# Moving part of a kernel's transposes from TensorE to the DMA crossbar: K and Q from pair 5 on, u from batch 1 on

## The chip, the cores and the metric

The kernel runs on one core of a Trainium2 chip. The metric is the device time of one execution in microseconds (us), the median of several runs; lower is better. The kernel before takes 288.5 us (three runs, 288.3 to 289.1). On one core a run is called slow when it is over 1.5% above the fastest of its kernel.

## The reference, cut to what matters

```python
# batch 4, 8 heads, 768 positions, head size 64; d_model 512, d_tok 256, d_ch 1536
scores = q @ k.transpose(0, 1, 3, 2) / 8        # block-sparse mask, softmax over keys
x = softmax(where(mask, scores, -1e9)) @ v      # heads put side by side: 768 x 512 per batch
h = relu(x.T @ w_tok1) @ w_tok2                 # token mixing
u = x + h.T
out = u + relu(u @ w_ch1) @ w_ch2               # channel mixing
```

## The kernel before

Two heads form a pair; there are 16 pairs, four to a batch. QK names the matmuls of the scores, PV those of the softmax with v; the exponentials between them run on ScalarE. Each pair's K and Q arrive with positions on the partitions, and the QK matmuls read them with the head dimension there, so they are transposed: 12 TensorE transposes a pair into PSUM (the memory that the matmuls write), then four copies (evacuations) to SBUF on VectorE or ScalarE. The same is done for u: 24 transposes and four copies a batch. Rows 64 to 87 of the `ktb` and `qtb` tiles hold a mask in low-rank form, which QK adds to the scores.

```python
qtb = [sb1.tile([128, S], BF16, name=f"qtb{n}") for n in range(2 * NV)]   # NV = 4 pairs in flight
ktb = [sb1.tile([128, S], BF16, name=f"ktb{n}") for n in range(2 * NV)]
# ... cut ...
def transposes(p):
    # ... cut: relayout(p) copies the loaded raw tiles into klay and qlay ...
    for nm, bufs, there in (("k", ktb, kT_there), ("q", qtb, qT_there)):
        for c in range(NC):                         # NC = 6 blocks of 128 positions
            def emit(nm=nm, c=c, box=box, rel=rel):
                # ... cut ...
                nc.tensor.matmul(out=box["t"][:, c, :], lhsT=lays[nm][:, c, :, :]...,
                                 rhs=ident[:, :], is_transpose=True, ...)
        for hd in range(2):
            def evac(eng, ...):                     # 64 x 768 out of PSUM, on DVE or ACT
                ...
```

The kernel orders its own instructions. A small planner runs while the program is built. It holds a planned cost for each instruction and a planned landing time for each DMA, plays the engines against each other, and at each step emits the instruction of best priority that would be ready by then. The emitted order is fixed: on the chip each engine takes its instructions in that order and waits at whichever is not ready, even if a later one is.

The softmax here doesn't subtract the row's maximum and nothing guards it: scores larger than these inputs give would overflow.

Of the kernel before, what the change touches and what calls it, by code (L numbers as in the profile page):

```python
# [50 lines left out]
class Planner:  # L51
# [11 lines left out]
    def __init__(self, slots):  # L63
        self.now = 0.0
        self.free_at = {"pe": 0.0, "act": 0.0, "dve": 0.0}
        self.streams = []
        self.ops = []
        self.count = 0
        self.slots = {tag: [Ev(0.0)] * n for tag, n in slots.items()}
        self.exp_pending = 0  # L70
# [6 lines left out]
    def op(self, engines, cost, deps, emit, prio=5, lat=60.0):  # L77
        done = Ev()
        self.ops.append((prio, self.count, engines, cost, deps, emit, done, lat))
        self.count += 1  # L80
        return done
# [21 lines left out]
    def step(self):  # L103

        nxt = []
        moved = False
        if self.free_at["pe"] <= self.now:
            for s in self.streams:
                while s[3] is None or (callable(s[3]) and s[3]()):
                    s[3] = next(s[2], False)  # L110
                if s[3] is False or callable(s[3]):
                    continue
                cost, deps, tags, emit, done = s[3]
                t = self.when(deps, tags)
                if t is None:
                    continue
                if t <= self.now:
                    s[3] = None
                    emit()
                    if self.trace is not None:  # L120
                        self.trace.append((self.now, "pe", s[0], cost))
                    self.free_at["pe"] = self.now + cost
                    if done is not None:
                        done.t = self.now + cost + self.PE_LAT + self.SEM
                    moved = True
                    break
                nxt.append(t)
            self.streams = [s for s in self.streams if s[3] is not False]
        else:
            nxt.append(self.free_at["pe"])  # L130
        for eng in ("act", "dve"):
            if self.free_at[eng] > self.now:
                nxt.append(self.free_at[eng])
                continue
            best = None
            for o in self.ops:
                prio, num, engines, cost, deps, emit, done, lat = o
                if eng not in engines:
                    continue
                if eng == "act" and prio > 0 and self.exp_pending:  # L140
                    continue
                t = self.when(deps)
                if t is None:
                    continue
                if t <= self.now:
                    if best is None or (prio, num) < best[:2]:
                        best = o
                else:
                    nxt.append(t)
            if best is not None:  # L150
                prio, num, engines, cost, deps, emit, done, lat = best
                self.ops.remove(best)
                emit(eng)
                c = cost[eng]
                if self.trace is not None:
                    self.trace.append((self.now, eng, prio, c))
                self.free_at[eng] = self.now + c
                done.t = self.now + c + lat + self.SEM
                moved = True
        if moved:  # L160
            return True
        later = [t for t in nxt if t > self.now]
        if not later:
            return False
        self.now = min(later)
        return True
# [3 lines left out]
def kernel(  # L170
# [22 lines left out]
    NET = 8  # L193

# [14 lines left out]
    qtb = [sb1.tile([128, S], BF16, name=f"qtb{n}") for n in range(2 * NV)]  # L209
    ktb = [sb1.tile([128, S], BF16, name=f"ktb{n}") for n in range(2 * NV)]  # L210

    P = Planner({"ps": 2, "po": 1, "pm": 3, "et": NET, "a_t": 2, "o": 3, "rc": 2,
                 "lay": 2, "kq": NV, "va": NV})
# [112 lines left out]
    rows_there = {("k", n): Ev() for n in range(2 * NV)} | {("q", n): Ev() for n in range(2 * NV)}  # L326

    def mask_stream():
# [15 lines left out]
        for h in range(2):  # L344
            def copy(eng, h=h):
                nc.scalar.copy(out=qtb[0][R, 384 * h : 384 * h + 384], in_=pms[h][R, 0:384])
            e2.append(P.op(("act",), {"act": 420.0}, [done], copy, prio=0))
            rels[h].same_as = e2[h]
        rows_there["q", 0].same_as = e2[1]
        for n in range(2 * NV):  # L350
            for nm, bufs in (("k", ktb), ("q", qtb)):
                if (nm, n) == ("q", 0):
                    continue

                def copy(eng, n=n, nm=nm, bufs=bufs):
                    nc.vector.tensor_copy(
                        out=bufs[n][R, :], in_=indf if nm == "k" else qtb[0][R, :]
                    )
                rows_there[nm, n].same_as = P.op(
                    ("dve",), {"dve": 300.0}, e2, copy, prio=2 if n < 2 else 6  # L360
                )
# [5 lines left out]
    ones_there = [Ev() for _ in range(NV)]  # L367

# [14 lines left out]
    def relayout(p):  # L383
        lays = {}
        for nm in ("k", "q", "v"):
# [3 lines left out]
            def emit(eng, nm=nm, raw=raw):  # L389
                if nm == "v":  # L390
                    nc.vector.tensor_copy(out=vaug[p % NV][:, :, :, 0:64], in_=raw[:, :, :, :])  # L391
                    return
                lay = sbw.tile([128, NC, 2, D], BF16, tag=f"{nm}lay", bufs=2, name=f"{nm}lay{p}")
                nc.vector.tensor_copy(  # L394
                    out=lay[:, :, :, :], in_=raw[:, :, :, :].rearrange("p h c d -> p c h d")
                )
                lays[nm] = lay
# [4 lines left out]
            if nm != "v" and p >= 2:  # L402
                deps.append(qT_there[p - 2, 1])
# [4 lines left out]

    def transposes(p):
        for hd in range(2):  # L410
            kT_there[p, hd], qT_there[p, hd] = Ev(), Ev()
        yield lambda: ("v", p) in raws
        lays = relayout(p)
        for nm, bufs, there in (("k", ktb, kT_there), ("q", qtb, qT_there)):
# [15 lines left out]
            n_left = [2]  # L430
            for hd in range(2):
                buf = bufs[2 * (p % NV) + hd]

                def evac(eng, hd=hd, buf=buf, box=box):
                    i = box["t"][64 * hd : 64 * hd + 64, :, :].rearrange("p c s -> p (c s)")
                    if eng == "act":
                        nc.scalar.copy(out=buf[0:64, :], in_=i)
                    else:
                        nc.vector.tensor_copy(out=buf[0:64, :], in_=i)  # L439
# [17 lines left out]
    def qk_stream():  # L457
        for s in steps:
# [4 lines left out]
            def emit(s=s, done=done, rel=rel):  # L463
# [4 lines left out]
                for hd in range(2):  # L468
                    n = 2 * (p % NV) + hd
                    nc.tensor.matmul(  # L470
                        out=ps[:, hd, 0:384], lhsT=ktb[n][0:88, 128 * j : 128 * j + 128],
                        rhs=qtb[n][0:88, 384 * half : 384 * half + 384], start=True, stop=True,
# [3 lines left out]
                def exp(eng):  # L476
# [13 lines left out]
                [e for hd in range(2) for e in (  # L490
                    kT_there[p, hd], qT_there[p, hd],
                    rows_there["k", 2 * (p % NV) + hd], rows_there["q", 2 * (p % NV) + hd],
# [8 lines left out]
    def pv_stream():  # L501
        for s in steps:
# [3 lines left out]
            def emit(s=s, done=done):  # L506
# [23 lines left out]
                def norm(eng):  # L530
                    if b not in xs:
                        xs[b] = sbw.tile([128, NC, DM], BF16, tag="x", bufs=B, name=f"x{b}")
# [3 lines left out]
                        out=free(xs[b][:, 3 * half, 128 * pb : 128 * pb + 128], 0,  # L536
                                 [[64, 2], [DM, 3], [1, 64]]),
# [29 lines left out]

    def tok(b, g):
# [3 lines left out]
        for t in range(2):  # L572
            for sc in range(NC):
                def emit(t=t, sc=sc):
                    if t == 0 and sc == 0:
# [4 lines left out]
                        rhs=xs[b][:, sc, 256 * g : 256 * g + 256],  # L580
# [4 lines left out]
        if b not in st:  # L585
            st[b] = dict(u=xs[b], uT_there=[Ev() for _ in range(4)])
# [6 lines left out]
        for s2 in range(3):  # L593
# [16 lines left out]
            def add(eng, s2=s2, ubox=ubox):  # L610
                nc.vector.tensor_tensor(  # L611
                    out=st[b]["u"][:, 2 * s2 : 2 * s2 + 2, 256 * g : 256 * g + 256],
                    in0=ubox["pm"][:, :, :],
                    in1=xs[b][:, 2 * s2 : 2 * s2 + 2, 256 * g : 256 * g + 256], op=ALU.add,
# [5 lines left out]
        alias(a_rel, last)  # L620
        for dmc in (2 * g, 2 * g + 1):
            last, rel, tbox = Ev(), Ev(), {}
            for sc in range(NC):
                def emit(sc=sc, dmc=dmc, rel=rel, tbox=tbox):
                    if sc == 0:
                        P.take("pm", rel)
                        tbox["pt"] = psM.tile([128, NC, 128], BF16, tag="pm", name=f"pm_ut_{b}_{dmc}")
                    nc.tensor.matmul(  # L628
                        out=tbox["pt"][:, sc, :], lhsT=st[b]["u"][:, sc, 128 * dmc : 128 * dmc + 128],
                        rhs=ident[:, :], start=(sc == 0), stop=(sc == NC - 1), is_transpose=True,  # L630
                    )
                yield 56.0, [u_evs[sc // 2]], [("pm", 1)] if sc == 0 else [], emit, last if sc == NC - 1 else None

            def evac(eng, dmc=dmc, tbox=tbox):
                if "uT" not in st[b]:
                    st[b]["uT"] = sbw.tile([128, 4, S], BF16, tag="uT", bufs=B, name=f"uT{b}")
                o, i = st[b]["uT"][:, dmc, :], tbox["pt"][:, :, :].rearrange("p c s -> p (c s)")
# [9 lines left out]
    def ch(b, pool, tag):  # L647
# [4 lines left out]
        for cc in range(12):  # L652
            for sh in range(2):
                last, rel, pbox = Ev(), Ev(), {}
                for dmc in range(4):
                    first = dmc == 0
                    def emit(cc=cc, sh=sh, dmc=dmc, rel=rel, pbox=pbox):
                        if dmc == 0:
# [7 lines left out]
                            rhs=st[b]["uT"][:, dmc, 384 * sh : 384 * sh + 384],  # L666
# [11 lines left out]
                rc_there[cc, sh] = ev  # L678
        for sc in range(NC):
# [12 lines left out]
            def fin(eng, sc=sc, pbox=pbox):  # L692
                o = sbw.tile([128, DM], FP32, tag="o", bufs=3, name=f"o{b}_{sc}")
                nc.vector.tensor_tensor(  # L694
                    out=o[:, :], in0=pbox["pm"][:, :], in1=st[b]["u"][:, sc, :], op=ALU.add
# [37 lines left out]
    P.stream(-1, mask_stream())  # L733
    tok2_op = P.op(("dve",), {"dve": 900.0}, [tok2_raw], wtok2_lay, prio=3)
# [57 lines left out]
```

## Time and profile before

| | before |
|---|---|
| time | 288.5 us |
| span of the profiled run | 287.1 us |
| first exponential to last (ScalarE) | 12.0 to 160.9 us |
| last QK matmul to the last matmul | 159.7 to about 283 us |
| TensorE, ScalarE, VectorE busy | 94%, 67%, 45% |

The groups of instructions of the kernel before follow (line, engine, operation, tiles, shapes, count; then busy us and mean ns of one; then idle time of the engine before them and what ended it). The transposes and their copies are many small pieces, and exponentials and QK are the large groups of the attention stage.

```profile
L478 ACT ACTIVATE et<-ps 128x768 bf16<-128x768 f32 x192 | 143.2, 810 | 4.2 <-PE ps L470 3.2
...
L439 DVE COPY ktb<-tk 64x768 bf16<-64x768 bf16 x29 | 16.0, 552 | 17.5 <-PE tk L421 17.2
...
L421 PE MATMUL tq<-ident,qlay 128*128 128x128 bf16 x96 | 11.3, 230 | 0.2 <-DVE qlay L394 0.2
```

### The profile page before, as it was taken

How to read it: one execution, taken by the hardware profiler on the slowest of the kernel's cores; microseconds unless marked ns; L12 is line 12 of the kernel's file. 1: busy time of each engine (PE TensorE's matmuls, PEld its weight loads, DVE VectorE, ACT ScalarE, POOL GpSimd, SP SyncE). 2: the span in 40 equal slices, each digit the busy share in tenths (PEclk: the TensorE clock that was granted, in tenths of full speed). 3: DMA queues.
4: the chain of work that ended last, by engine and by line, in shares of the span. 5: the costliest groups of instructions: out<-in, count | busy, mean ns of one | idle time of the engine just before them, and what ended most of it. 6: DMA issues, size and time to landing. Idle time of an engine off the chain costs nothing.

```text
span 287.1 us, 6351 instructions
## 1 busy us (share of the span) xinstructions
PE 269.9 (94%) x2682; PEld 175.5 (61%) x2690; DVE 130.2 (45%) x286; ACT 191.9 (67%) x286; POOL 45.0 (16%) x70
## 2 busy tenths in 40 slices
PE   0799899999999999999999999999999999999994
PEld 0366676678777777777777754456544654456441
DVE  5789966557777569765546341210022001200121
ACT  1589999999999999999999642037501770067200
POOL 7956554522211000000000000000000000000000
PEclk9999999999999999999999999999999999999999
DMA  4999999996254100000000001220022001210122
GB/s 55 134 204 202 214 201 205 201 185 87 39 73 66 23 2 2 0 2 3 2 0 2 2 0 39 106 76 0 2 110 84 29 0 73 94 54 0 38 102 82
DMA packets 19168, 20.07 MB, mean 70 GB/s; under 512 B 1348, under 2 KB 15428, under 8 KB 19140
## 3 DMA queue, kind: packets, MB, share of 16 engines
q0 software_dynamic: 15648, 13.37, 30.3%
q1 hardware_dynamic: 3492, 6.29, 5.8%
q8 instruction: 21, 0.34, 0.5%
q14 instruction: 7, 0.06, 0.1%
HBM read 26.74 MB, written 6.29 MB: 115 GB/s over the span
## 4 chain that ended last, share of the span: by engine, by line
PE 73%; ACT 14%; DVE 6%; issue 2%; DMA 2%; POOL 2%; POOLq 0%; DVEq 0%; ACTq 0%
PE pm_ch L686 22%; PE pm_ch L664 21%; ACT et L478 14%; PE ps L470 14%; PE po L520 8%; PE pm_tok L578 3%; PE pm_tok L603 2%; DMA kraw<-in_k_dram 2%; DVE qtb L439 1%; PE pm_ut L628 1%; PE tq L421 1%; DVE ktb L439 1%; PE tk L421 1%; DVE x L535 1%; DVE klay L394 1%
## 5 line engine op out<-in xcount | busy, mean ns | idle before, releaser
L478 ACT ACTIVATE et<-ps 128x768 bf16<-128x768 f32 x192 | 143.2, 810 | 4.2 <-PE ps L470 3.2
L470 PE MATMUL ps<-qtb,ktb 88*128 88x384 bf16 x384 | 95.3, 329 | 4.0 <-ACT et L478 1.7
L560 ACT ACTIVATE rc<-pm_ch 128x384 bf16<-128x384 f32 x84 | 41.2, 491 | 60.7 <-PE pm_ch L664 44.8
L520 PEld LDWEIGHTS <-et 128*128 128x128 bf16 x1152 | 56.0, 97 | 22.8 <-DVE x L535 1.9
L664 PE MATMUL pm_ch<-uT,w_ch 128*128 128x384 bf16 x384 | 68.6, 326 | 0.2 <-DVE rc L562 0.2
L686 PE MATMUL pm_ch<-w_ch,rc 128*128 128x512 bf16 x280 | 62.4, 379 | 0.4
L520 PE MATMUL po<-vaug,et 128*128 128x65 bf16 x1152 | 61.5, 193 | 0.5 <-ACT et L478 0.2
L694 DVE TENSOR_TENSOR o<-pm_ch,x 128x512 f32<-128x512 f32 x24 | 16.6, 692 | 98.7 <-PE pm_ch L686 98.7
L664 PEld LDWEIGHTS <-w_ch 128*128 128x128 bf16 x384 | 37.0, 98 | 23.1 <-issue 0.3
L686 PEld LDWEIGHTS <-rc 128*128 128x128 bf16 x288 | 28.2, 98 | 33.6
L470 PEld LDWEIGHTS <-ktb 88*128 88x128 bf16 x384 | 34.2, 99 | 11.9 <-issue 4.4
L439 DVE COPY ktb<-tk 64x768 bf16<-64x768 bf16 x29 | 16.0, 552 | 17.5 <-PE tk L421 17.2
L611 DVE TENSOR_TENSOR x<-pm_tok,x 128x512 bf16<-128x512 f32 x24 | 16.2, 687 | 6.8 <-PE pm_tok L603 6.5
L535 DVE TENSOR_TENSOR x<-po,recip 128x384 bf16<-128x384 f32 x32 | 17.8, 557 | 1.1
L439 DVE COPY qtb<-tq 64x768 bf16<-64x768 bf16 x30 | 16.6, 552 | 2.1 <-PE tq L421 1.1
L603 PE MATMUL pm_tok<-a_t,w_tok 128*128 128x256 bf16 x96 | 17.0, 272 | 0.0
L230 POOL DMA_DIRECT2D vraw<-in_v_dram x16 | 12.3, 766 | 28.4 <-DVE vaug L391 25.7
L578 PE MATMUL pm_tok<-x,w_tok 128*128 128x256 bf16 x96 | 16.3, 272 | 0.0
L230 POOL DMA_DIRECT2D kraw<-in_k_dram x16 | 11.6, 727 | 7.7 <-DVE recip L534 2.2
L230 POOL DMA_DIRECT2D qraw<-in_q_dram x16 | 11.5, 720 | 6.4 <-DMA w_ch<-in_moe_w_ch_dram 2.4
L534 DVE RECIPROCAL recip<-po 128x6 f32<-128x6 f32 x32 | 6.2, 195 | 12.0 <-PE po L520 11.6
L421 PE MATMUL tq<-ident,qlay 128*128 128x128 bf16 x96 | 11.3, 230 | 0.2 <-DVE qlay L394 0.2
(49 smaller groups left out, 122.8 us busy)
## 6 DMA issues: line engine op xcount, KB each, us to landing
out_dram<-o SPq DMA_DIRECT2D x24, 256.0 KB, 2.0
kraw<-in_k_dram POOLq DMA_DIRECT2D x16, 192.0 KB, 7.9
qraw<-in_q_dram POOLq DMA_DIRECT2D x16, 192.0 KB, 7.4
vraw<-in_v_dram POOLq DMA_DIRECT2D x16, 192.0 KB, 7.0
w_ch<-in_moe_w_ch_dram POOLq DMA_DIRECT2D x8, 384.0 KB, 9.8
w_tok<-in_moe_w_tok_dram POOLq DMA_DIRECT2D x1, 384.0 KB, 7.8
w_tok2r<-in_moe_w_tok_dram POOLq DMA_DIRECT2D x1, 384.0 KB, 9.0
samp<-in_sampled_blocks_dram SPq DMA_DIRECT2D x1, 0.6 KB
```

The source lines that it names most:

```text
L230: nc.gpsimd.dma_start(out=raw[:, :, :, :], in_=APx(src, 2 * p * S * D, [[NC * D, 128], [S * D, 2], [1, NC * D]]),)
L421: nc.tensor.matmul(out=box["t"][:, c, :], lhsT=lays[nm][:, c, :, :].rearrange("p h d -> p (h d)"), rhs=ident[:, :], start=(c == 0), stop=( ...
L439: nc.vector.tensor_copy(out=buf[0:64, :], in_=i)
L470: nc.tensor.matmul(out=ps[:, hd, 0:384], lhsT=ktb[n][0:88, 128 * j : 128 * j + 128], rhs=qtb[n][0:88, 384 * half : 384 * half + 384], star ...
L478: nc.scalar.activation(out=et[:, :, :], in_=ps[:, :, 0:384], func=AF.Exp, scale=0.125)
L520: nc.tensor.matmul(out=po[:, hd, c, :], lhsT=et[:, hd, 128 * c : 128 * c + 128], rhs=va[:, hd, j, 0:65], start=(j == 0 and hd == 0 and c = ...
L535: nc.vector.tensor_tensor(out=free(xs[b][:, 3 * half, 128 * pb : 128 * pb + 128], 0, [[64, 2], [DM, 3], [1, 64]]), in0=po[:, :, :, 0:64], ...
L560: nc.scalar.activation(out=o(), in_=i, func=AF.Relu)
L578: nc.tensor.matmul(out=box["pm"][:, t, :], lhsT=w_tok1[:, sc, 128 * t : 128 * t + 128], rhs=xs[b][:, sc, 256 * g : 256 * g + 256], start=( ...
L603: nc.tensor.matmul(out=ubox["pm"][:, i, :], lhsT=w_tok2[:, t, 2 * s2 + i, :], rhs=a_t[:, t, :], start=(i == 0 and t == 0), stop=(i == 1 an ...
L664: nc.tensor.matmul(out=pbox["pm"][:, 0:384], lhsT=w_ch1[:, dmc, 128 * cc : 128 * cc + 128], rhs=st[b]["uT"][:, dmc, 384 * sh : 384 * sh + ...
L686: nc.tensor.matmul(out=pbox["pm"][:, :], lhsT=box["rc"][:, cc, 128 * sc : 128 * sc + 128], rhs=w_ch2[:, cc, :], start=(cc == 0), stop=(cc ...
```

## The change

The intent is to take 204 of the 288 transposes off the full TensorE and their evacuations off VectorE. For pairs 5 to 15 VectorE copies the raw K (and Q) into a "wide" tile whose blocks are 128 columns: 64 of data, 24 of mask constants, 40 of zeros. One crossbar transfer (`dma_start_transpose`, a DMA that transposes on its way) then writes all of `ktb` (or `qtb`) of the pair. There are two wide tiles for each of K and Q, so pair p+2 uses pair p's tiles again. For batches 1 to 3 a crossbar transfer turns each half of u. All 28 transfers are issued by SyncE. The early pairs stay on TensorE; in the kernel before, the input loads fill the DMA engines up to about 65 us (DMA share 1.17 to 1.28 in the windows from 10 to 60 us, 0.67 from 60 to 80, 0.35 from 80 to 100). The core of the diff, cut:

```diff
+    NPE = 5
+    NL = 2
-    qtb = [sb1.tile([128, S], BF16, name=f"qtb{n}") for n in range(2 * NV)]
-    ktb = [sb1.tile([128, S], BF16, name=f"ktb{n}") for n in range(2 * NV)]
+    qtb = [sb1.tile([128, 2, S], BF16, name=f"qtb{n}") for n in range(NV)]
+    ktb = [sb1.tile([128, 2, S], BF16, name=f"ktb{n}") for n in range(NV)]
+    wide = {
+        (nm, n): sb1.tile([128, 2, NC, 128], BF16, name=f"{nm}wide{n}")
+        for n in range(NL) for nm in ("k", "q")
+    }
 ... (relayout)
+                elif p >= NPE:
+                    nc.vector.tensor_copy(out=wide[nm, p % NL][:, :, :, 0:64], in_=raw[:, :, :, :])
 ...
+            if nm != "v" and p >= NPE:
+                deps.append(wide_there[nm, p % NL])
+                if p - NL >= NPE:
+                    deps.append(xb_done[nm, p - NL])
 ...
+    def crossbar(p):
+        lays = relayout(p)
+        for nm, bufs, there in (("k", ktb, kT_there), ("q", qtb, qT_there)):
+            def emit(eng, nm=nm, bufs=bufs):
+                nc.sync.dma_start_transpose(
+                    out=bufs[p % NV][:, :, :].rearrange("e h (c s) -> e (h c) s", c=NC),
+                    in_=wide[nm, p % NL][:, :, :, :].rearrange("p h c e -> p (h c e)"),
+                )
+            deps = [lays[nm + "ev"]]
+            if p >= NV:
+                deps.append(qk_done[p - NV])
+            ev = P.op(("sp",), {"sp": 1500.0}, deps, emit, prio=1, lat=2500.0)
+            xb_done[nm, p] = ev
+            there[p, 0], there[p, 1] = ev, ev
 ... (tok: u)
+        if b > 0:
+            turn_by_crossbar(b, g, u_evs)
+            return
```

The numbers 1500 and 2500 are the planner's own ns for issue and landing of one transfer. The layouts of x, u and uT change with it, so that each half of u is contiguous.

## The prediction

> **What bounds the kernel now.** I read the page's slices first, to see where each engine is busy, then the table of stretches, then groups of instructions, then the order of instructions in time at the places where a stretch looked odd.
>
> The slices of the kernel before, 7.2 us each:
> ```profile
> PE   0799899999999999999999999999999999999994
> DVE  5789966557777569765546341210022001200121
> ACT  1589999999999999999999642037501770067200
> PEclk9999999999999999999999999999999999999999
> DMA  4999999996254100000000001220022001210122
> ```
> TensorE is full from slice 5 to the end at full clock. ScalarE is full only up to about 160 us (the softmax exponentials), the DMA engines only up to about 65 us. So there are two stages: attention, where TensorE and ScalarE are both full, and a tail of channel mixing, where TensorE is alone. The stretches say the same (columns: busy us and instructions of each engine, granted clock, DMA share, GB/s):
> ```profile
> 20.00:40.00 20.00, 18.35 (x244) 13.15 (x244) 17.33 (x40) 19.00 (x26) 11.12 (x16) 1.00 1.22 205
> ...
> 120.00:140.00 20.00, 19.75 (x274) 15.06 (x273) 11.76 (x25) 19.94 (x28) 0.00 (x0) 1.00 0.01 2
> ...
> 180.00:200.00 20.00, 19.95 (x109) 10.58 (x109) 2.77 (x4) 7.37 (x15) 0.00 (x0) 1.00 0.17 66
> ```
> Busy times overlap, so the cost on TensorE is the distance from one start to the next. The order in time on TensorE shows it (start us, length us, ... count):
> ```profile
> 162.34 1.47 PE L578 MATMUL pm_tok<-x,w_tok 128*128 128x256 bf16 x12
> ...
> 167.25 0.61 PE L628 MATMUL pm_ut<-ident,x 128*128 128x128 bf16 x8
> 168.06 6.01 PE L664 MATMUL pm_ch<-uT,w_ch 128*128 128x384 bf16 x36 [0.20 <-DVE rc L562]
> ```
> Eight transposes in 0.61 us of which the last one's 0.219 us is drain: (0.61-0.219)/7 = 56 ns each. In the same way 162.5 ns for a channel-mixing matmul of 384 columns ((6.01-0.326)/35), 109 ns for a token-mixing one of 256, and from like stretches 216 ns for 512 columns, 162 for a QK matmul, 29 for a PV matmul.
>
> In attention, which of the two is ahead? The exponentials' starts are 722 ns apart when nothing holds them (the fourth pair of heads: 12 in 8.68 us), but pairs 6 to 15 take 8.8 to 9.1 us each, 9.03 in the mean: TensorE paces there, by about 0.37 us a pair. In the first 60 us it is the other way round: of TensorE's idle time most lies there, waiting for ScalarE. One hole is worth naming, in ScalarE's order in time:
> ```profile
> 29.79 2.26 ACT L478 ACTIVATE et<-ps 128x768 bf16<-128x768 f32 x3
> 31.96 1.61 ACT L437 COPY ktb<-tk 64x768 bf16<-64x768 bf16 x2
> 33.91 0.80 ACT L437 COPY qtb<-tq 64x768 bf16<-64x768 bf16 x1 [0.33 <-DVE qtb L439]
> 34.99 18.51 ACT L478 ACTIVATE et<-ps 128x768 bf16<-128x768 f32 x25 [0.29 <-PE ps L470]
> ```
> For 2.95 us no exponential runs. VectorE's order in time tells why: the mask row of pair 2's second q buffer, a low-priority copy, is written only at 34.17 us behind the evacuations of later pairs' transposes, and the first QK of pair 2 starts at 34.34.
>
> [...]
>
> **The change part by part.** Numbers of instructions are from the two programs' instruction orders.
>
> Removed from TensorE: 12 transposes for each of 11 pairs (5 to 15) and 24 for each of 3 batches: 132 + 72 = 204, at 56 ns 11.4 us. Added: 12 small matmuls (24 columns) that make the constant columns of the wide tiles, some 0.4 us. Net 11.0 us of TensorE work of 257.6 (all matmuls at the distances above).
>
> Removed from VectorE and ScalarE: 4 evacuations a pair and 4 a batch, 44 + 12 = 56, at 552 ns 31 us, nearly all VectorE's, which isn't the bound. Added there: 4 clears and 4 copies, planned at 420 and 450 ns, 3.5 us around 30 to 40 us. The re-layout copies (371 ns) stay, with another destination.
>
> Moved: the kernel orders its matmuls with a planner of its own, and fills the freed time in attention with channel mixing. After the last QK matmul the program before has 345 first-layer and 288 second-layer channel matmuls, 24 token matmuls, 12 transposes and 18 PV matmuls: 345x0.1625 + 288x0.216 + 24x0.109 + 12x0.056 + 18x0.029 = 122.1 us; the trace has 159.7 to about 283, 123.4 us. The changed program has 288, 278, 24, 0 and 18: 46.8 + 60.0 + 2.6 + 0.5 = 110.0 us. So the tail is 12.1 us shorter by its order alone, unless attention grows.
>
> Attention: its work on TensorE is 1.0 us more than before (136.5 against 135.5), as 57 + 10 channel matmuls (11.4 us) replaced the transposes. By pair:
> - pair 0: same order but for small things, 10.9 us as before.
> - pair 1: before 12.06 us with the hole. In the changed order pair 2's mask rows stand before pair 1's first normalization, and ScalarE evacuates nothing after its first two copies, so the hole should be gone. TensorE has 7.4 us of work; ScalarE's 8.7 rule, with VectorE still crowded: 9.3.
> - pairs 2 to 4: 7.7 to 8.2 us of TensorE work, so ScalarE's pace: 8.75 each, 26.25 (before 26.7).
> - pair 5: 8.57 us of work, 8.85.
> - pairs 6 to 14: 8.99 and 8.87 us of work in turn. The loss over 60 to 160 us is now 3.8 us, 0.34 a pair, part of it at the changes between transposes and QK; I take 0.28: 9.2 each, 82.8. Pair 15: 9.0.
>
> First exponential at 12.0 as before; 12.0 + 10.9 + 9.3 + 26.25 + 8.85 + 82.8 + 9.0 = 159.1, against 160.9 before. The last QK is 1.2 us earlier, 157.9. Tail 110.0 plus 0.6 of waits (before 1.3, with the wait on u's transposes, which goes): 268.5. From there to the end of the measured time it is 288.47 - 283.1 = 5.4 us before, the same after: 273.9. I say 274.2, leaving a little for crossbar disturbance.
>
> Do the crossbar transfers hide? Pair p may start once QK of pair p-4 is done, some 27 us ahead of its use. Batch 3's u is used only after batches 1 and 2, over 60 us later. So latency is hidden; only throughput matters: 22 + 4 transfers between about 35 and 147 us, one per 4.3 us.
>
> **The rivals.**
> 1. The crossbar is slower than one transfer per 4.3 us. The DMA packets of the trace before take 79 ns for 768 B and 86 ns for 2 KB, almost flat: if a transpose goes as 1536 rows of 256 B at some 60 ns over 16 engines, it takes 5.8 us (my estimate), 26 take 150 us where 112 are there, QK waits, and the time goes to 300 us or more. For it: the flat cost. Against it: [...] the kernel's own plan counts 1.5 us of issue and 2.5 of landing, where its other costs (552 against 550 planned, 692 against 695) match the trace closely.
> 2. Loads collide. DMA share is over 1.2 of the page's measure until 65 us, and the first crossbars (pairs 5 to 7) fall into 35 to 50 us. Loads or transposes late by a few us would still be met by the 27 us lead; if not, one stall of 2 to 5 us, 276 to 279.
> 3. ScalarE takes over: it cannot go below 8.66 us a pair, so what TensorE gains in attention beyond the fill is idle. The plan's fill leaves TensorE at 8.9 a pair, so little is lost. If attention kept its length exactly, the time would be 288.5 - 12.1 = 276.4.
> 4. The strided reading of the new u transposes (three runs of 128 columns) slows 384 channel matmuls. [...] At 5% it would cost 3 us.
>
> **Range and chances.** Rivals 2 to 4 give 274 to 279, a cleaner attention stage 271.5. Predicted 274.2 us, 271 to 279. Faster by over 2% (below 282.7) 0.90; within 2% 0.04; slower by over 2% 0.06, nearly all rival 1.
>
> **What would show it.** Right: no exponential gap between pairs 1 and 2; pairs 6 to 14 at about 9.2 us; end of the exponentials near 159; tail from last QK of about 110.5 us; transposes landing within a few us. Wrong: TensorE waiting for a DMA into ktb, qtb or uT; pairs above 9.5 us; channel matmuls with a distance above 163 ns.

The forecast's sum: 159.1 us to the end of the exponentials, so the last QK at 157.9; with 110.0 + 0.6 for the tail 268.5; with 5.4 to the end 273.9, said as 274.2. There is no term for a crossbar transfer in it, since I took the transfers as hidden. What stands against rival 1 is the planner's own 1.5 and 2.5 us; the trace before has no crossbar transfer, so no measured transfer stood against it. The 60 ns of rival 1 is an estimate of mine, set below the 79 and 86 ns that it stands beside. The 0.4 us for the 12 small matmuls was an estimate too; in the trace after they take 0.38 us (36.57 to 36.95).

## More of the kernel before

The chain of work that ended last, by engine, as a share of the span. DMA is almost absent from it:

```profile
PE 73%; ACT 14%; DVE 6%; issue 2%; DMA 2%; POOL 2%; POOLq 0%; DVEq 0%; ACTq 0%
```

## The result, and the profile after

The changed kernel takes 303.6 us (four runs: 301.5, 303.2, 304.0, and 310.3, which counts as slow) against 288.7 us (its four runs). Ratios here and below are the mean time of one kernel's fast runs over that of the other's of the same rounds, so not quite the ratio of the medians: 1.049, interval 1.043 to 1.055. The prediction was 274.2 us with a range to 279: wrong, and in the wrong direction.

The slices of the kernel after, 7.5 us each:

```profile
PE   0799993249897995989999999999999999999994
...
DVE  5689870124462642553545342420012001210021
ACT  1679993219897994889999998006710572047300
...
PEclk9999998559999998899999999999999999999998
DMA  3999999999999997853952002151012101210022
```

TensorE has a hole at slices 6 to 8 (45 to 68 us) and smaller dents up to slice 17, in places where it was full before. ScalarE and VectorE have the hole too, so none of the three was working: they all waited for something else. The only row that is full there is DMA, and it stays full to about 113 us, where before it ended at 65. From slice 18 on the picture is as hoped.

The chain that ended last, by engine, has DMA with 18% of the span where it had 2%:

```profile
PE 67%; DMA 18%; ACT 6%; DVE 4%; POOL 2%; issue 1%; SPq 0%; POOLq 0%; DVEq 0%; ACTq 0%
```

The instructions in order of time on VectorE show who waited (start us, length us, engine, line, operation, tiles, count, then idle time before it and what ended it):

```profile
44.12 0.67 DVE L694 TENSOR_TENSOR x<-pm_tok,x 128x512 bf16<-128x512 f32 x1
55.35 0.36 DVE L432 COPY kwide<-kraw 128x768 bf16<-128x768 bf16 x1 [10.56 <-DMA ktb<-kwide]
55.63 0.68 DVE L694 TENSOR_TENSOR x<-pm_tok,x 128x512 bf16<-128x512 f32 x1
63.53 0.36 DVE L432 COPY qwide<-qraw 128x768 bf16<-128x768 bf16 x1 [7.21 <-DMA qtb<-qwide]
63.80 0.19 DVE L597 RECIPROCAL recip<-po 128x6 f32<-128x6 f32 x1
```

The copy of pair 7's K into its wide tile stands in VectorE's order between two additions for token mixing. It must wait until pair 5's transfer has read the same tile, and so VectorE stands still for 10.6 us, then 7.2 us for Q. The addition and the normalization (the reciprocal) behind the copies were wanted by others. TensorE's order in time in the same stretch:

```profile
47.31 0.28 PE L715 MATMUL pm_ut<-ident,x 128*128 128x128 bf16 x2
56.37 0.29 PE L715 MATMUL pm_ut<-ident,x 128*128 128x128 bf16 x1 [8.78 <-DVE x L694]
...
64.64 0.84 PE L583 MATMUL po<-vaug,et 128*128 128x65 bf16 x12 [6.59 <-DVE x L598]
```

TensorE waits 8.8 us for the addition, then 6.6 us for the normalization, whose PSUM buffer PV needs. Nobody here waits for a `ktb` or `qtb` tile to be filled. Over the whole run VectorE waits 38 us for K and Q transfers, by the view of waits (us in total, times, longest):

```profile
DVE kwide L432 <- DMA ktb<-kwide: 21.0, 6, 10.6
DVE qwide L432 <- DMA qtb<-qwide: 17.0, 6, 7.2
```

Why were the transfers late? SyncE's order in time shows the issues (the length is how long SyncE's queue was held by one issue):

```profile
41.13 4.13 SPq L461 DMA_TRANSPOSE ktb<-kwide  x1
45.32 8.58 SPq L461 DMA_TRANSPOSE qtb<-qwide  x1
54.00 7.71 SPq L461 DMA_TRANSPOSE ktb<-kwide  x1
61.76 5.54 SPq L461 DMA_TRANSPOSE qtb<-qwide  x1
```

The view of the tile qtb between 40 and 62 us, and that of ktb between 128 and 152 us, end with the time from issue to landing of the transfers in that stretch:

```profile
DMA to landing us min/median/max: 11.8/14.9/18.1
```
```profile
DMA to landing us min/median/max: 3.8/3.8/3.8
```

The same transfer lands after 12 to 18 us early on and after 3.8 us later. The profile page's part on DMA queues says what was added (packets, MB, share of 16 engines); q1 carried only the outputs before, 3,492 packets and 5.8%:

```profile
q1 hardware_dynamic: 47396, 17.31, 30.7%
q0 software_dynamic: 15648, 13.37, 29.3%
```

The added 43,008 packets of 256 B are 28 transfers of 1,536 packets each. I counted the packets by start time in the trace's DMA records:

```
stretch of the kernel after   crossbar packets (256 B)   load packets (1024 or 768 B)
45 to 48 us                    449                        461
48 to 51                       476                        453
54 to 57                       562                        560
57 to 60                       586                        550
60 to 63                       560                        556
163 to 168, no loads          1536 in 2.03 us               0
```

In these stretches the two queues go one packet for one. A load packet of 768 B takes 78 ns and one of 1,024 B 96 ns, a crossbar packet 30 ns there (18 in the median without loads, from 163 to 168 us), so a transfer gets some 150 to 195 packets through in a us and lasts 8 to 10 us in place of 2.0: 9.2 and 8.0 us for the first two, from the first packet to the last. The rest of the 12 to 18 us is waiting: the first transfer's packets start 4.0 us after its issue, the second's at 54.3 us, 9.0 us after its issue and right behind the first's last packet. These are counts; that the engines take turns is read from them, and no run varies the turns themselves.

By pairs of heads, from a pair's first exponential to the next pair's, I read the cost of it in the trace:

| pair | before | predicted | after |
|---|---|---|---|
| 0 | 10.9 | 10.9 | 11.7 |
| 1 | 12.1 | 9.3 | 9.1 |
| 2 | 9.0 | 8.75 | 9.3 |
| 3 | 8.7 | 8.75 | 26.4 |
| 4 | 9.0 | 8.75 | 9.0 |
| 5 | 8.9 | 8.85 | 10.4 |
| 6 | 9.0 | 9.2 | 11.2 |
| 7 | 9.1 | 9.2 | 9.5 |
| 8 | 9.1 | 9.2 | 14.5 |
| 9 | 9.0 | 9.2 | 10.1 |
| 10 to 14, mean | 9.0 | 9.2 | 9.05 |

The exponentials end at 187.9 us, 28.8 later than predicted. Pair 3 has 17.6 of that, pairs 5 to 9 another 10. The tail, from the last QK at 186.6 to the end of the last matmul at 297.6, is 111.0 us, as predicted. The last channel-mixing stretches on TensorE look like this:

```profile
204.01 15.76 PE L753 MATMUL pm_ch<-uT,w_ch 128*128 128x384 bf16 x96
```

(15.76 - 0.326)/95 = 162.5 ns between matmuls, the same as before, so the strided reading of the new uT costs nothing.

### The profile page after: what moved, and what is told of

Its sections match the earlier page's. It is cut to its first block, busy times and chain, and to the rows that moved or that the text cites. A ratio compares the mean times of both kernels' runs of the same rounds, so it can differ in the third digit from the quotient of the medians.

```text
span 301.5 us, 6014 instructions
## 1 busy us (share of the span) xinstructions
PE 263.5 (87%) x2498; PEld 167.0 (55%) x2498; DVE 112.0 (37%) x254; ACT 184.5 (61%) x270; POOL 44.8 (15%) x70
## 4 chain that ended last, share of the span: by engine, by line
PE 67%; DMA 18%; ACT 6%; DVE 4%; POOL 2%; issue 1%; SPq 0%; POOLq 0%; DVEq 0%; ACTq 0%
PE pm_ch L776 21%; PE pm_ch L753 19%; PE ps L533 14%; DMA qtb<-qwide 13%; PE po L583 8%; ACT et L542 6%; PE pm_tok L686 3%; DMA qraw<-in_q_dram 2%; DMA ktb<-kwide 2%; PE pm_tok L661 2%; DMA kraw<-in_k_dram 2%; DVE x L598 1%; DVE qwide L432 1%; POOL kraw L236 1%; POOL vraw L236 0%
## 5 line engine op out<-in xcount | busy, mean ns | idle before, releaser
L533 PE MATMUL ps<-qtb,ktb 88*128 88x384 bf16 x384 | 98.6, 339 | 3.0 <-ACT qtb L500 1.6
L583 PEld LDWEIGHTS <-et 128*128 128x128 bf16 x1152 | 57.9, 99 | 38.7 <-DVE x L598 16.3
L583 PE MATMUL po<-vaug,et 128*128 128x65 bf16 x1152 | 63.3, 196 | 13.3 <-DVE x L598 13.3
L753 PE MATMUL pm_ch<-uT,w_ch 128*128 128x384 bf16 x384 | 72.3, 326 | 0.0
L625 ACT ACTIVATE rc<-pm_ch 128x384 bf16<-128x384 f32 x72 | 35.4, 491 | 55.6 <-PE pm_ch L753 55.5
L776 PE MATMUL pm_ch<-w_ch,rc 128*128 128x512 bf16 x288 | 64.6, 379 | 0.0
L533 PEld LDWEIGHTS <-ktb 88*128 88x128 bf16 x384 | 36.1, 101 | 16.2 <-issue 4.7
L694 DVE TENSOR_TENSOR x<-pm_tok,x 128x512 bf16<-128x512 f32 x24 | 15.8, 684 | 12.5 <-PE pm_tok L686 12.5
L236 POOL DMA_DIRECT2D vraw<-in_v_dram x16 | 12.1, 755 | 39.8 <-DVE vaug L430 29.3
L627 DVE TENSOR_SCALAR rc<-pm_ch 128x384 bf16<-128x384 f32 x24 | 13.2, 553 | 11.2 <-PE pm_ch L753 11.1
L432 DVE COPY kwide<-kraw 128x768 bf16<-128x768 bf16 x11 | 4.0, 368 | 21.0 <-DMA ktb<-kwide 21.0
L432 DVE COPY qwide<-qraw 128x768 bf16<-128x768 bf16 x11 | 3.9, 355 | 19.7 <-DMA qtb<-qwide 17.0
## 6 DMA issues: line engine op xcount, KB each, us to landing
w_ch<-in_moe_w_ch_dram POOLq DMA_DIRECT2D x8, 384.0 KB, 10.1
```

The source lines that it names most:

```text
L236: nc.gpsimd.dma_start(out=raw[:, :, :, :], in_=APx(src, 2 * p * S * D, [[NC * D, 128], [S * D, 2], [1, NC * D]]),)
L533: nc.tensor.matmul(out=ps[:, hd, 0:384], lhsT=ktb[n][0:88, hd, 128 * j : 128 * j + 128], rhs=qtb[n][0:88, hd, 384 * half : 384 * half + 38 ...
L583: nc.tensor.matmul(out=po[:, hd, c, :], lhsT=et[:, hd, 128 * c : 128 * c + 128], rhs=va[:, hd, j, 0:65], start=(j == 0 and hd == 0 and c = ...
L625: nc.scalar.activation(out=o(), in_=i, func=AF.Relu)
L694: nc.vector.tensor_tensor(out=st[b]["u"][:, g, 2 * s2 : 2 * s2 + 2, :], in0=ubox["pm"][:, :, :], in1=xs[b][:, g, 2 * s2 : 2 * s2 + 2, :], ...
L753: nc.tensor.matmul(out=pbox["pm"][:, 0:384], lhsT=w_ch1[:, dmc, 128 * cc : 128 * cc + 128], rhs=st[b]["uT"][:, dmc // 2, 3 * sh : 3 * sh + ...
```

## The experiments

My theory after this reading has two parts. A: a late transfer stops VectorE, which stands at a refill of a wide tile, and VectorE's stop stops everyone. D, which the texts name from `e5` on: the loads make the transfers late, packet by packet. The rivals: B, the crossbar's own throughput is the bound, whoever waits; C, the opening is spoiled by the new layouts or by the preparation of the wide tiles; E, the crossbar traffic disturbs the engines' memory access. Eleven kernels ran, ten with correct results and `e9` wrong; all were timed in three rounds, `e10` in five.

### e1_wide4: four wide tiles in place of two

```diff
+    NW = 4
-        for n in range(NL) for nm in ("k", "q")
+        for n in range(NW) for nm in ("k", "q")
-    wide[nm, p % NL] ... wide_there[nm, p % NL]
+    wide[nm, p % NW] ... wide_there[nm, p % NW]
-                o = sbw.tile([128, DM], FP32, tag="o", bufs=3, ...)
+                o = sbw.tile([128, DM], FP32, tag="o", bufs=2, ...)
```

> Edit: the changed kernel with four wide buffers for each of K and Q in place of two (and two output buffers in place of three to make room); order of the planner and all 28 crossbar transfers kept. Theory A (VectorE, in order, stands before the copy that refills a wide buffer until an earlier crossbar transfer has landed, 38 us in the changed kernel, and normalizations and u additions behind it stand too): those VectorE waits on K and Q transfers drop from 38 us to under 8, the 9.3 and 7.3 us gaps of the exponentials in pair 3 go; what is left is QK of pairs 5 to 7 waiting for late landings, 5 to 8 us: time 278 to 284. Rival B (the crossbar's own throughput is the bound, whoever waits for it): QK waits in VectorE's place, time 297 or more.

Measured: 288.1 us, ratio to before 0.997 (0.993 to 1.002): 15.5 us better than the changed kernel, but not the 278 to 284 expected. The gap in pair 3 is gone (8.9 us). VectorE still waits 18.8 us in all for K and Q transfers, and there is a wait that the changed kernel did not have. From the view of waits of this run (engine, line waited for: us in total, times, longest):

```profile
DVE qwide L433 <- DMA qtb<-qwide: 14.2, 4, 5.3
...
PE ps L534 <- DMA qtb<-qwide: 5.9, 2, 3.3
...
DVE kwide L433 <- DMA ktb<-kwide: 4.6, 1, 4.6
```

QK of pair 5 starts at 63.66 us, right behind the landing of pair 5's Q at 63.52; QK of pair 6 at 79.20, behind 79.07. So about half of the loss goes with two more wide tiles. VectorE's first stops, in pair 3, go; what is left comes later, and now QK also waits, because the transfers themselves are too late: the first four land at 55.6, 63.5, 72.3 and 79.1 us, some 8 us apart, where the pairs need two in 9 us. Rival B is right under the loads, and only there: after 110 us this run's transfers land after 4 to 6 us.

### e4_plan_late: only the planned landing time changed

```diff
-            ev = P.op(("sp",), {"sp": 1500.0}, deps, emit, prio=1, lat=2500.0)
+            ev = P.op(("sp",), {"sp": 1500.0}, deps, emit, prio=1, lat=14000.0)
```

> Edit: one number in the kernel's own plan, the landing time that it counts for a K or Q transfer, from 2.5 to 14 us; instructions and transfers the same, only their order differs (the copies that refill wide buffers stand later in VectorE's order). Theory A: the early waits of VectorE (10.6 and 7.2 us) shrink to under 4 us together, time 280 to 290. Rival B (throughput of the crossbar under the loads): no gain, within 2% of the changed kernel's 303.

Measured: 292.7 us, ratio 1.014 (1.011 to 1.017). The same instructions in another order (their counts on each engine are equal in the two traces) are 11 us faster than the changed kernel, so the order alone around the late landings was worth that much. The gap moved rather than vanished: pair 3 takes 8.9 us, but VectorE stops for 6.3, 5.1 and 5.8 us between 57 and 77 us, and pairs 4 and 5 take 14.4 and 21.6 us:

```profile
DVE qwide L432 <- DMA qtb<-qwide: 12.1, 2, 6.3
DVE kwide L432 <- DMA ktb<-kwide: 5.1, 1, 5.1
```

The expected under 4 us of early waits was missed, and the time fell just outside the expected 280 to 290.

### e2_pairs9: the crossbar only from pair 9 on

```diff
-    NPE = 5
+    NPE = 9
```

> Edit: pairs 5 to 8 go back to TensorE, crossbar for K and Q from pair 9 on (u as in the changed kernel). Transfers then start near 70 us, when the input loads thin out. Theory A plus contention with loads: landings take 4 to 7 us in place of 12 to 18, VectorE waits under 6 us, 48 transposes more on TensorE (2.7 us), tail 112.3 us by its order: time 275 to 280. Rival B (crossbar throughput whatever the loads do): landings stay over 8 us, 14 + 6 transfers still stop VectorE, time 290 or more. Rival C (loss is in the opening, from the new layouts or the preparation of the wide tiles): time stays near 300.

Measured: 282.7 us, ratio 0.981 (0.976 to 0.986), faster than before (the interval holds both sides of 2%, so the verdict at that size is unclear) but over the expected 275 to 280. The K and Q transfers start at 67.6 us and land after 3.8 to 6.7 us. VectorE still waits 11.3 us in all for them, where under 6 were expected. Rival C falls, since the wide tiles are prepared here too. One larger stop is left, near 76 us, seen in ScalarE's order in time:

```profile
79.47 0.81 ACT L542 ACTIVATE et<-ps 128x768 bf16<-128x768 f32 x1 [3.58 <-PE ps L533]
```

It lies behind a 2.8 us wait of VectorE for pair 9's Q, which landed 6.7 us after issue while the plan counted 2.5.

### e3_u_only: K and Q on TensorE, u by the crossbar

```diff
-    NPE = 5
+    NPE = 16
-    P.stream(-1, wide_stream())
   (one wide tile, four uT tiles; whichever half of u comes first makes the tile)
```

> Edit: all K and Q transposes on TensorE, only u of batches 1 to 3 by the crossbar (wide tiles and their preparation left out, four uT buffers). Six transfers, none near the loads, no copy on VectorE waits for a landing. Theory A: no VectorE wait on a transfer; 72 transposes less on TensorE (4.0 us), tail by its order 118.3 against 122.1: time 284 to 286 (0.985 to 0.99). Rival C (the new layouts of x, u and uT cost time): 289 or more, with channel matmuls over 163 ns apart.

Measured: 281.2 us, ratio 0.974 (0.973 to 0.976), better than expected. Six transfers, landing after 3.6 to 5.7 us, stop nobody. Of the 7.4 us gained, 3.8 are the shorter tail by its order (118.3 against 122.1 us), and the exponentials end 2.8 us earlier, at 158.1, mostly because the hole between pairs 1 and 2 is closed (pair 1 takes 9.0 us in place of 12.1).

### e5_ch2_late: one load moved

```diff
-        if p == 7:
+        if p == 12:
             loads.append(load_ch2)
```

> Edit: the changed kernel with one load moved: the four 384 KB loads of the second channel weights are issued after pair 12's loads in place of after pair 7's (they are used only after 185 us). Theory D (packet by packet, a crossbar transfer of 1536 packets of 256 B takes turns with the loads' packets, one for one, so it lasts 8 to 10 us while a load runs and 2.8 us without): the loads behind these come forward into the same time, so the first two landings stay about 8 us apart, but the crossbars meet fewer load packets before 66 us in all and the loads' end comes some 9 us earlier: 294 to 300 in place of 303. If the weights' own packets (1024 B, 96 ns) were what made it slow, first landings would come within 8 us of issue: 285 or less.

Measured: 303.2 us, ratio 1.052 (1.046 to 1.058). The expected gain did not come. (The one for one of the expectation is the count in the changed kernel's trace, 562 packets against 560 in 3 us; its 2.8 us without a load was an estimate, where a lone transfer there took 2.0.) The loads of the weights were simply met by other transfers, in ScalarE's order in time:

```profile
55.16 1.56 ACT L542 ACTIVATE et<-ps 128x768 bf16<-128x768 f32 x2 [8.38 <-PE ps L533]
...
99.43 0.81 ACT L542 ACTIVATE et<-ps 128x768 bf16<-128x768 f32 x1 [10.11 <-PE ps L533]
```

The first gap shrank from 9.3 + 7.3 us to 8.4 + 3.1, but a new one of 10.1 us appeared: the weights now land between 81 and 89 us, and pair 9's transfers, issued at 79.5 and 84.2, land after 14.2 and 12.5 us. The stall follows the loads. This speaks for D, and it shows why moving one load does not help as long as transfers are in flight whenever a load can be.

### e6_dummies: the disputed cost by itself

```diff
   (on e3_u_only: six transfers that nobody reads)
+    for when in (41, 125):
+        for n in range(3):
+            def idle(eng, n=n):
+                nc.sync.dma_start_transpose(out=spare[n]..., in_=wide["k", 0]...)
+            P.op(("sp",), {"sp": 1500.0}, [cleared, Ev(when * US)], idle, prio=0, lat=2500.0)
```

> Edit: the u-only run (281.2) with six idle crossbar transfers of the same size from a cleared tile into tiles that nobody reads: three issued near 30 to 41 us, under the loads, three near 120 us, after them. It measures the disputed cost by itself, with nobody waiting. Theory D: early ones land 8 to 13 us apart (the loads' packets are 768 and 3072 B there), late ones 2.6 to 3.2 us apart; the time stays within 0.7% of the u-only run's. Rival B (the transfer is slow by itself): early and late alike. Rival E (crossbar traffic disturbs the engines' memory access): the time grows by 1% or more though nobody waits.

Measured: 288.8 us, ratio 1.001 (0.999 to 1.003), 7.5 us slower than `e3_u_only`. The early three land at 47.5, 57.8 and 65.9 us, 8 to 10 us apart; of the later ones two have a recorded landing, 4.6 and 4.1 us after issue. That part of D held, with nobody waiting for these transfers. The time did not stay within 0.7%, which by the letter of the expectation speaks for rival E; but pairs 5 to 15 take 9.03 us in the mean here and in `e3_u_only`, with transfers under way or not. What grew is pair 4 (14.7 us against 9.0) and, by 1.2 us, the tail, with seven more channel matmuls after the last QK in the planner's order. VectorE's order in time of this run:

```profile
53.50 0.69 DVE L694 TENSOR_TENSOR x<-pm_tok,x 128x512 bf16<-128x512 f32 x1
58.64 0.36 DVE L435 COPY klay<-kraw 128x768 bf16<-128x768 bf16 x1 [4.45 <-DMA kraw<-in_k_dram]
```

VectorE stands 4.5 us before the copy of pair 8's K, which the plan had put there because its load should have been in. That load lands at 58.6 us here and at 52.1 in `e3_u_only`. So the taking of turns works both ways: the early transfers pushed the loads back by 6.5 us, and a late load stops VectorE just as a late transfer does. By 58.6 us 3,370 crossbar packets had started, 2.2 transfers; at some 30 ns each over 16 engines that is 6.3 us, an estimate that fits. The three transfers after 127 us delayed nothing.

### e9_no_loads: the loads taken away

Wrong result on purpose.

```diff
+            if p >= 8:                                # raw tiles of pair p-4 used again, nothing loaded
+                raws[nm, p], arrive[nm, p] = kept[nm, p - 4], Ev(t)
+                kept[nm, p] = raws[nm, p]
+                continue
-        for i in range(4):                            # second channel weights
+        for i in range(1):
-                        rhs=w_ch2[:, cc, :], ...
+                        rhs=w_ch2[:, cc % 3, :], ...
```

> Wrong result on purpose. Edit: the changed kernel, crossbar from pair 5 on, two wide buffers, but from pair 8 on nothing is loaded (the raw tiles of pair p-4 are used again) and only a quarter of the second channel weights is. All transposes, copies and matmuls stay; from about 46 us on no load packet competes. Theory D (the loads' packets make the transfers late, the late transfers stop VectorE, and all of the loss comes of it): only the first transfer or two late (landing 8 to 10 us after issue), the rest 4 to 6 us; exponential gaps under 3 us together after 42 us; the time comes to what was predicted for the change, 273 to 277. If the structure itself is at fault (two wide buffers, 28 transfers on one queue), it stays above 285.

Measured: 280.8 us, ratio 0.972 (0.970 to 0.974). Same change, same 28 transfers, two wide tiles: 22.8 us of the loss of 29.4 (303.6 against the predicted 274.2) go with the loads. VectorE's order is nearly that of the changed kernel (243 of its 254 instructions stand at the same place), so the reordering by the planner is no rival here. It stayed over the expected 273 to 277, though. ScalarE's order in time shows what is left:

```profile
49.59 1.56 ACT L548 ACTIVATE et<-ps 128x768 bf16<-128x768 f32 x2 [2.92 <-PE ps L539]
...
109.04 56.24 ACT L548 ACTIVATE et<-ps 128x768 bf16<-128x768 f32 x74 [1.79 <-PE ps L539]
```

Pair 3 still takes 13.2 us, since the first transfer meets the last loads before 46.4 us and lands after 8.2 us, and VectorE stands 4.7 us. Pair 9 takes 10.8: with no loads at all a Q transfer next to one of u lands after 6.5 us, over the 2.5 that the plan counts. In both VectorE stands at a refill placed too early; in pair 3 the last loads still have a part in it.

### e7_pairs9_wide4 and e8_pairs11_late: two versions that follow from this

```diff
   e7: NPE = 9, four wide tiles (as e1), planned landing 4500 in place of 2500
   e8: NPE = 11, second channel weights loaded after pair 12 (as e5), planned landing 4500, two wide tiles
```

> Edit: crossbar for K and Q from pair 9 on, four wide buffers in place of two, landing planned at 4.5 us in place of 2.5. Against the run with pair 9 alone (282.7, where VectorE still stood 2.8 us before a refill and the exponentials stopped 3.6 us): no VectorE wait on a landing above 1 us, no exponential gap above 1 us: time 276.5 to 279. If the stop near 76 us was not from the refill but from QK or the tok stage, 282 stays.

> Edit: crossbar for K and Q from pair 11 on only, second channel weights loaded after pair 12, landing planned at 4.5 us; two wide buffers. Theory D: transfers start after 85 us with few loads left, landings of 4 to 6 us; 60 K and Q transposes and 72 of u less on TensorE than before; tail by its order 114.9; attention as in the u-only run (158): 277.5 to 280.

Measured: `e7` 276.6 us (276.4 to 276.8), ratio 0.959 (0.957 to 0.960); `e8` 278.5 us, ratio 0.965 (0.964 to 0.967). Both as expected. In `e7` no wait of VectorE on a landing is left, and ScalarE runs from 39.5 us to the last exponential without a gap of note:

```profile
39.46 119.03 ACT L543 ACTIVATE et<-ps 128x768 bf16<-128x768 f32 x158
```

It beats both kernels: 27 us faster than the changed one and 12 us faster than the one before.

### e10_pairs8_wide4: one pair more

```diff
   on e7: NPE = 8, planned landing 6500
```

> Edit: as the best run so far (four wide buffers, 276.6 with pair 9), crossbar from pair 8 on and landing planned at 6.5 us. 12 transposes less on TensorE, 0.7 us; two more transfers, issued near 58 us while loads run until about 69 us. Theory D: if their lateness stays inside the lead of 27 us, 275.5 to 276.5; if the loads they push back reach VectorE's copies, a stop of 1 to 3 us and 277 to 279.

Measured: six runs from 275.2 to 281.1 us, ratio of the fast ones 0.961 (0.957 to 0.965); three of the six count as slow. The 275.2 is the best single time, but the kernel is not steady, while `e7` stays within 0.4 us. The profiled run (a slow one) has transfers from 58 us on that land after 14 to 22 us, up to 101 us, long after `e7` has landings of 4 to 9.5. I found no cause for that. It is not the number of very long packets: crossbar packets of over 1 us, which a lone transfer has none of, number 135 of 33,792 here, but 170 of 30,720 in the steady `e7`. The loads do reach to 99 us in that trace, but the turns of one for one do not describe it: from 75 to 91 us there are 179 crossbar packets a us beside 76 of the loads, and both kinds take longer (80 and 112 ns in the mean, against 30 and 78 in the changed kernel from 54 to 63 us). `e1`, in a fast run, has such a stretch too (84 to 91 us: 210 and 57 a us, 58 and 152 ns). What makes the packets longer there stays open. Which of the two versions is faster in its good runs is not settled by this.

### e11_rows_first: the hole between pairs 1 and 2 by itself

```diff
   on the kernel before
-                    ("dve",), {"dve": 300.0}, e2, copy, prio=2 if n < 2 else 6
+                    ("dve",), {"dve": 300.0}, e2, copy, prio=2 if n < 6 else 6
```

> Edit: the kernel before, no crossbar, with one priority changed: the mask rows of pairs 1 and 2 are copied before the evacuations of later pairs. It measures the hole of 2.95 us between pairs 1 and 2 by itself, which the changed kernel and all its variants are without. Hole closed, nothing else changed: 285 to 286 (0.988 to 0.991). If the gain of the variants over the count of removed transposes has another source, 288.

Measured: 286.9 us, ratio 0.994 (0.993 to 0.996). Pair 1 takes 8.9 us in place of 12.1, so the hole is closed as the prediction read it, but only 1.8 us of the 3 arrive, short of the expected 285 to 286: the first exponential starts 0.2 us later and some other pairs take a little longer (pair 7 9.3 us, pair 13 9.25); that the earlier row copies are the reason is not shown. So some 2 us of what the crossbar variants gain come from a better order and not from the crossbar.

## Why the prediction was wrong

**What held.** The reading of what bounds the kernel and the cost of a transpose were right. The tail was predicted at 110.6 us and came to 111.0. Pairs 10 to 14 were predicted at 9.2 us and took 9.05. The hole between pairs 1 and 2 went, with 9.1 us for pair 1 against 9.3. The strided reading of u (rival 4) cost nothing (162.5 ns between channel matmuls, as before). Where its premise was restored, the gain came: with the crossbar from pair 9 on and nothing waiting, `e7` gains 12 us, some 2 of them from the order (`e11`). One slip did not matter: for the 5.4 us after the last matmul the prediction took the trace of a run of 288.84 us from a median of 288.47; with that run's own time it is 5.8.

**The step that failed** is in "Do the crossbar transfers hide?": "Pair p may start once QK of pair p-4 is done, some 27 us ahead of its use. [...] So latency is hidden; only throughput matters". The 27 us are the lead of QK over the transfer. But a transfer has a second waiter, which I did not look for: VectorE's copy that refills the same wide tile for pair p+2. Its lead is only what the planner gave, 1.5 + 2.5 us, as it was placed in VectorE's order right behind the planned landing. VectorE then held up additions and normalizations that had nothing to do with the transfer. The runs show this by the order alone (`e4`, 11 us) and by the number of wide tiles (`e1`, 15.5 us, with one output tile less to make room).

**The second failing step** is in rival 2: "Loads or transposes late by a few us would still be met by the 27 us lead; if not, one stall of 2 to 5 us, 276 to 279." The lateness was mis-sized: 12 to 18 us from issue to landing and 8 us from landing to landing, where the prediction has only the planner's 1.5 us of issue and 2.5 of landing, against a need of one transfer per 4.3 us. At 8 us the throughput misses that need, so in the loaded stretch rival 1 came true as well, as `e1` shows, where QK waits 5.9 us. That rival 1 named "300 us or more" and 303.6 was measured is luck: its path, QK waiting, is in no wait of the changed kernel. The lead was mis-sized too: in `e1` pair 5's Q is issued at 44.8 us, held behind its K, and QK stands for it from 60.4 us on, 15.6 us later and not 27; it landed after 18.8. I had the number of packets right in rival 1 (1,536 of 256 B), but priced them as if they were alone (60 ns, my estimate; measured 18 in the median alone, 30 under loads), and in rival 2 I did not ask how a queue of small packets shares an engine with a queue of large ones. The trace of before does not show it, as it has no crossbar packets. But I could have asked what one packet for one would come to: from the 79 ns of a 768 B packet in that trace and my 60 ns, 1536 x (79 + 60)/16 = 13 us for a transfer under a load (an estimate; the runs show 8 to 10), which is too much for both waits.

**The size of the loss.** Of 29.4 us over the prediction, `e9` ties 22.8 to the loads. Of the 6.6 us left, pair 3 has some 4, where the first transfer still meets loads, and pair 9 some 2, where the plan's landing time is too short without any. How much of the loss is VectorE's standing and how much is the late data cannot be added up neatly, because removing one lets the other through.

**Left open.** The changed kernel varies by 3% between runs and `e10` by 2%, where the kernel before varies by 0.3%, and no run tells why. Nor is it known what made both kinds of packets longer in `e10`, and in `e1` from 84 us on. TensorE's granted clock also fell during the long holes (0.67 in the mean from 42 to 68 us); what that added was not measured apart.

## What to carry to other kernels

When work moves to the DMA engines, list every instruction that waits for the transfer, also the one that writes its source again, and ask what stands behind that one on an engine that takes its instructions in order; the slack that counts is the smallest of these. In the loaded stretches measured here small packets went one for one with large ones, so that a transfer took 8 to 10 us in place of 2.0 (562 packets against 560 in 3 us of the changed kernel), and the loads were held up in turn (6.5 us in `e6`); start such transfers where the loads are over. A kernel with a planner is only as good as its planned landing times, and a change in one of those numbers (`e4`) is a cheap test of it.

Figures of these runs that may help with the next estimate:

- A lone crossbar transfer of 393 KB (1,536 packets of 256 B) takes 2.03 us from its first packet to its last, 194 GB/s (changed kernel, 164.3 to 166.3 us), and lands 3.8 us after issue. Under loads, 8 us from landing to landing is 49 GB/s; from first packet to last it is 8.0 to 9.2 us against 2.0, some four times longer.
- How many packets an engine takes in one turn the counts do not tell.
- Beside other traffic the issue itself took longer: one transpose held SyncE's queue for 1.4 us without loads (changed kernel, K transfers from 128 to 152 us), for 4.1 us under them with no transfer before it (the first, at 41.13 us), and for up to 10.2 us under them behind another transfer (`e6_dummies`).
- In a stream one block of 128x128 took 56 ns on TensorE (before) and 169 ns by a lone crossbar transfer (2.03 us for 12 blocks); the evacuation, which in these kernels only TensorE's way has, took 552 ns for each six half blocks.
